# Tanh to SBUF buffers of its own in a fused attention and gated convolution kernel, with a mask on TensorE, three weight loads, halved V shifts and a new order

## The chip, the cores and the metric

The kernel runs on one core of a Trainium2 chip. The metric is device time in microseconds (us). Runs of one kernel differ (those of the kernel before lay between 226.52 and 231.59 us), so each version was run several times beside the kernel before, on the same chip. A run counts as slow if it is over 1.5% above the fastest of the same kernel. "Granted clock" is the share of full speed that TensorE's clock was given.

In the profile PE is TensorE's matmuls, PEld its weight loads, DVE is VectorE, ACT is ScalarE, POOL is GpSimd and SP is SyncE, which issues the DMAs.

## The reference

Eight batches, eight heads, 576 positions, head size 64: attention in a window of 32 to each side, then a feed-forward layer with a depthwise convolution of three taps along the sequence and a gate.

```python
scores = scale * q @ k.T                  # kept where abs(i - j) <= 32
x = (softmax(scores) @ v)                 # heads side by side: 8 x 576 x 512
h = np.maximum(x @ w_in, 0.0)             # 8 x 576 x 1024
conv_out = sum(conv_w[k] * hp[:, k:k + S, :] for k in range(3))
gate = 1.0 / (1.0 + np.exp(-conv_out))
out = h * gate @ w_out
```

Since 1/(1+exp(-x)) = (1 + tanh(x/2))/2, the kernel keeps hT = h/2 in bf16, convolves that, and forms (tanh + 1) * hT.

## The kernel before: the parts that matter

The sequence is cut into twelve chunks of 384 positions, each in eight tiles of 128 features. One chunk is cut into halves of 192, so there are 88 long units and 16 short ones, 104 in all. A unit goes: projection on TensorE into PSUM, relu into SBUF (hT), three taps shared out among TensorE, VectorE and GpSimd with the sum in a PSUM bank (pc, shown as pf in the profile), tanh on ScalarE, gate on VectorE into gT, output projection on TensorE.

```python
def emit_tanh(e_):                        # PSUM -> the same PSUM bank
    scalar.activation(pc.ap[:, 0:nc_], pc.ap[:, 0:nc_], AF.Tanh, bias=0.0, scale=1.0)

def emit_gate(e_):                        # (tanh + 1) * hT: one input in PSUM, one in SBUF
    vector.scalar_tensor_tensor(
        out=gT.ap[...], in0=in3(pc.ap), scalar=1.0, in1=taps(1), op0=ALU.add, op1=ALU.mult)
```

Two more kinds of VectorE instruction matter for the comparison, both with two inputs in SBUF: a tap that starts from a GpSimd product, and the mask of the attention.

```python
def emit_times(e_, cp, kk):               # GpSimd: cp = tap weight * hT, SBUF -> SBUF
    gpsimd.tensor_scalar(out=in3(cp.ap), in0=taps(kk), scalar1=w_tap(kk), ...)

def emit_tap(e_, kk, from_):              # VectorE: from_ is pc (PSUM) or cp (SBUF)
    vector.scalar_tensor_tensor(out=in3(pc.ap), in0=taps(kk), scalar=w_tap(kk), in1=in3(from_.ap), ...)

def emit_mask(e_, x=x):                   # VectorE or GpSimd: attn = attn * mask
    (vector if e_ == "V" else gpsimd).tensor_tensor(out=at_.ap[...], in0=at_.ap[...], in1=mask, op=ALU.mult)
```

All instructions are emitted in the order of one table, which names the engine and the buffer of each; filler matmuls on a tile of zeros are set into it at the start. The kernel uses eight PSUM banks, in turns. `cp` is GpSimd's tap buffer, `vo` is V shifted by 64 positions, `ve` V as loaded and cast, `qkb` the cast q and k, `xn` the normalised attention output.

The softmax here doesn't subtract the row's maximum and nothing guards it: scores larger than these inputs give would overflow.

## Time and profile before

| | before |
|---|---|
| time, median of 3 runs | 228.67 us (227.7 to 229.04) |
| span of the profiled run | 225.6 us |
| VectorE busy, GpSimd busy | 197.3 us, 137.7 us |
| the 104 gates | 52.1 us of VectorE |

```profile
PEld L232 <- DVE gT L232: 0.9, 2, 0.5
```

### The profile page before, as it was taken

Reading aid. Unit: us, or ns where it says so; the run is one execution under the profiler, and the core shown is the slowest. Engines: PE = TensorE matmul, PEld = TensorE weight load, DVE = VectorE, ACT = ScalarE, POOL = GpSimd, SP = SyncE. Lnnn points to the kernel's source line nnn. Section 1 sums busy time; section 2 is a strip of 40 time slices with the busy share of each in tenths; the row PEclk is TensorE's granted clock in tenths of the full one; section 3 lists DMA queues with packets and bytes.
Section 4 is the critical chain, followed back from the end, with each engine's and each line's share of the span. In section 5 each row is a group of like instructions: output and inputs, shape, how many; then the busy total and the mean of one; then the engine's idle time right before and its main releaser. Section 6 shows DMA issues by size and latency. Waiting matters only on the chain.

```text
span 225.6 us, 7189 instructions
## 1 busy us (share of the span) xinstructions
PE 211.5 (94%) x2720; PEld 122.9 (54%) x2720; DVE 197.3 (87%) x467; ACT 187.5 (83%) x474; POOL 137.7 (61%) x203
## 2 busy tenths in 40 slices
PE   7698899989989999989999998999999999999993
PEld 5366567658555655545555454545655565455541
DVE  6279869899999979797999788989999999899990
ACT  2689899998989889879889989689989999777642
POOL 5978654654376937695368736756386735566640
PEclk9889999999999999999999999999999999999999
DMA  6999999999989999999997989994535212501224
GB/s 201 331 285 358 355 266 281 321 308 253 290 170 324 317 175 287 236 306 224 288 347 129 202 278 358 182 231 147 144 36 118 99 46 49 175 1 49 93 101 178
DMA packets 66391, 48.16 MB, mean 214 GB/s; under 512 B 50781, under 2 KB 50805, under 8 KB 66357
## 3 DMA queue, kind: packets, MB, share of 16 engines
q1 hardware_dynamic: 64992, 46.32, 78.6%
q10 hardware_dynamic: 1364, 1.39, 2.9%
q8 instruction: 21, 0.34, 0.8%
q14 instruction: 14, 0.11, 0.2%
HBM read 32.52 MB, written 9.44 MB: 186 GB/s over the span
## 4 chain that ended last, share of the span: by engine, by line
PE 41%; DVE 18%; ACT 17%; DMA 13%; issue 5%; SPq 3%; POOL 2%; DVEq 0%; ACTq 0%; POOLq 0%
PE pf L232 41%; DMA st<-in_k_dram 7%; ACT attn L232 6%; DVE pf L232 5%; DVE gT L232 4%; SPq L232 3%; DMA out_dram<-y 3%; ACT xn L232 3%; DVE qkT L232 2%; ACT pf L232 2%; DMA vo<-ve 2%; DVE attn L232 2%; DVE xn L232 2%; ACT qkb L232 2%; ACT y L232 1%
## 5 line engine op out<-in xcount | busy, mean ns | idle before, releaser
L232 PE MATMUL pf<-xT,w_in_sb 128*128 128x385 bf16 (+2 forms) x416 | 73.4, 315 | 3.6 <-ACT hT L232 0.9
L232 PE MATMUL pf<-w_out_sb,gT 128*128 128x512 bf16 x288 | 72.2, 380 | 0.0
L232 POOL TENSOR_SCALAR cp<-hT,conv_w_sb 128x384 f32<-128x384 bf16 (+1 forms) x63 | 38.9, 622 | 46.1 <-ACT hT L232 20.2
L232 ACT ACTIVATE pf<-pf 128x384 f32<-128x384 f32 (+1 forms) x104 | 48.2, 477 | 13.1 <-DVE pf L232 11.1
L232 DVE SCALAR_TENSOR_TENSOR gT<-pf,hT 128x384 bf16<-128x384 f32 (+1 forms) x104 | 52.1, 517 | 5.5 <-ACT pf L232 5.1
L232 PEld LDWEIGHTS <-w_in_sb 128*128 128x128 bf16 x416 | 38.6, 98 | 27.8 <-issue 4.5
L232 ACT ACTIVATE attn<-pf 128x512 bf16<-128x512 f32 (+1 forms) x96 | 41.4, 522 | 1.8 <-PE pf L232 1.8
L232 ACT ACTIVATE hT<-pf 128x385 bf16<-128x385 f32 (+2 forms) x76 | 35.4, 487 | 6.0 <-PE pf L232 5.6
L232 PEld LDWEIGHTS <-gT 128*128 128x128 bf16 x288 | 26.0, 98 | 25.7 <-DVE gT L232 0.5
L232 DVE SCALAR_TENSOR_TENSOR pf<-hT,conv_w_sb,pf 128x384 f32<-128x384 bf16 (+1 forms) x61 | 34.7, 586 | 1.2 <-PE pf L232 1.1
L232 PE MATMUL pf<-hT,diag_w 128*128 128x384 bf16 (+1 forms) x153 | 30.9, 309 | 0.9 <-DVE xn L232 0.6
L232 POOL TENSOR_SCALAR qkb<-st 128x1152 bf16<-128x1152 f32 (+1 forms) x23 | 25.7, 1122 | 7.6 <-DMA st<-in_k_dram 3.2
L232 DVE COPY qkT<-pf 128x576 bf16<-128x576 bf16 x35 | 25.6, 750 | 4.9 <-PE pf L232 4.9
L232 POOL TENSOR_TENSOR cp<-cp,cp 128x384 f32<-128x384 f32 (+1 forms) x24 | 24.4, 1016 | 1.6
L232 DVE TENSOR_TENSOR attn<-attn,mask 128x1152 bf16<-128x1152 bf16 x26 | 23.0, 886 | 2.4 <-ACT attn L232 2.3
L232 ACT ACTIVATE xn<-pf,rec 128x64 bf16<-128x64 f32 x96 | 22.0, 360 | 1.5 <-DVE rec L232 1.5
L232 ACT COPY y<-pf 128x512 f32<-128x512 f32 x30 | 18.1, 605 | 3.9 <-PE pf L232 3.7
L232 DVE SCALAR_TENSOR_TENSOR pf<-hT,conv_w_sb,cp 128x384 f32<-128x384 bf16 (+1 forms) x35 | 21.2, 618 | 0.0
L232 POOL TENSOR_TENSOR attn<-attn,mask 128x1152 bf16<-128x1152 bf16 x6 | 14.2, 2371 | 8.4 <-ACT attn L232 8.4
L232 DVE TENSOR_TENSOR xn<-pf,rec 128x256 bf16<-128x256 f32 x48 | 18.9, 410 | 0.0
L232 ACT COPY qkT<-pf 128x576 bf16<-128x576 bf16 x29 | 18.6, 664 | 0.4 <-PE pf L232 0.2
L232 PEld LDWEIGHTS <-diag_w 128*128 128x128 bf16 x153 | 13.3, 97 | 9.8 <-issue 1.3
(49 smaller groups left out, 235.2 us busy)
## 6 DMA issues: line engine op xcount, KB each, us to landing
st<-in_q_dram SPq DMA_DIRECT2D x16, 576.0 KB, 6.8
out_dram<-y SPq DMA_DIRECT2D x36, 256.0 KB, 3.8
st<-in_k_dram SPq DMA_DIRECT2D x14, 576.0 KB, 8.2
vst<-in_v_dram SPq DMA_DIRECT2D x24, 256.0 KB, 7.0
vst<-in_v_dram SPq DMA_DIRECT2D x15, 192.0 KB, 5.7
vo<-ve SPq DMA_DIRECT2D x11, 260.0 KB, 5.6
st<-in_moe_w_in_dram SPq DMA_DIRECT2D x2, 1024.0 KB, 9.3
st<-in_moe_w_out_dram SPq DMA_DIRECT2D x2, 1024.0 KB, 9.4
```

Source lines behind the costliest of these rows:

```text
L232: return lambda *args, **kwargs: fixed(do(*args, **kwargs))
```

## The change

The intent is to free a PSUM bank at the tanh's end instead of at the gate's end, to take work off VectorE and GpSimd, and to shorten the start. The core of the diff:

```diff
-BUFS = {'st': 3, ..., 'rec': 4, 'xn': 3, 'hT0': 8, 'hT1': 6, 'hT2': 6, 'cp': 2, 'gT': 4, 'y': 7}
+BUFS = {'st': 4, ..., 'rec': 8, 'xn': 2, 'hT0': 7, 'hT1': 7, 'hT2': 7, 'cp': 2, 'gT': 3, 'y': 5, 'tn': 3}
+MASKS = ('aa', 'mm', 'mm', 'mm', 'mm', 'mm', 'mm', 'mm')
 (CONV, who computes which tap, TURNS and ORDER: new tables)
+    tn_p = pool("tn", [128, CH], FP32)
...
-            scalar.activation(pc.ap[:, 0:nc_], pc.ap[:, 0:nc_], AF.Tanh, bias=0.0, scale=1.0)
+            scalar.activation(tn.ap[:, 0:nc_], pc.ap[:, 0:nc_], AF.Tanh, bias=0.0, scale=1.0)
...
-                ..., in0=in3(pc.ap), scalar=1.0,
+                ..., in0=in3(tn.ap), scalar=1.0,
                 in1=taps(1), op0=ALU.add, op1=ALU.mult,
...
+                if added:                 # first batch: the mask is added to the scores on TensorE
+                    for n, e, width in ((2, x, 2), (0, 0, 8), (1, 1, 8)):
+                        tensor.matmul(ps[n].ap[...], outside[rows, :], ident[...], start=True, stop=False)
...
+    W_PARTS = {"in": ((0, 2), (2, 4), (4, MB)), "out": ((0, MB // 2), (MB // 2, MB))}
...
-        for c in range(NBLK - 1) if b < 2 else (0,):
-            shift_v(b, c, c + 1 if b < 2 else NBLK - 1)
+        for c in range(0, NBLK - 1, 1 if b < 2 else 2):
+            shift_v(b, c, c + (1 if b < 2 else 2))
```

## The prediction

What the prediction calls the lock is its assumption that a VectorE instruction with two SBUF inputs and a GpSimd instruction hold each other up. Of the trace of before it had the mask, which has two SBUF inputs: the ten masks that started with a GpSimd instruction running for 0.1 us or more took 1104 ns, the other 16 took 750. The gates, with one input in PSUM and one in SBUF, took 548 ns beside a GpSimd instruction (79 of the long ones) and 550 without (9). The rows by form bear on whether an SBUF source is quicker than PSUM, and the "starts 216 ns apart" are those of matmuls. On the blur that it mentions: of the 64-row matmuls of 64 columns, 498 of 1098 starts came under 5 ns after the one before.

> **What bounds the kernel now.** I read the page's busy shares first, then the windows by stage, the chain of waits, the groups by form, and last the order of time around single instructions. The busy shares:
>
> ```profile
> PE 211.5 (94%) x2720; PEld 122.9 (54%) x2720; DVE 197.3 (87%) x467; ACT 187.5 (83%) x474; POOL 137.7 (61%) x203
> ...
> DMA  6999999999989999999997989994535212501224
> ```
>
> No engine is idle on average, so the shares alone decide nothing; the stages do. The windows (length, then busy time of PE, PEld, DVE, ACT, POOL, then granted clock, DMA share and GB/s):
>
> ```profile
> 10.00:20.00 10.00, 9.68 (x177) 6.78 (x174) 7.37 (x12) 9.32 (x22) 8.07 (x18) 0.84 1.06 303
> 20.00:30.00 10.00, 8.89 (x124) 5.74 (x122) 8.27 (x27) 8.83 (x28) 7.41 (x9) 1.00 1.08 368
> ...
> 60.00:100.00 40.00, 37.80 (x575) 21.23 (x575) 37.00 (x88) 34.69 (x84) 29.79 (x29) 1.00 1.04 254
> 100.00:140.00 40.00, 38.12 (x536) 21.36 (x537) 35.01 (x83) 36.55 (x97) 24.21 (x29) 1.00 1.07 262
> 140.00:190.00 50.00, 50.00 (x634) 27.49 (x633) 48.84 (x110) 43.85 (x116) 30.66 (x38) 1.00 0.54 120
> 190.00:220.00 30.00, 29.50 (x155) 14.91 (x154) 28.52 (x56) 20.19 (x46) 16.94 (x24) 1.00 0.26 86
> ```
>
> Until about 26 us PE looks busy but mostly runs the 75 filler matmuls; ScalarE works through the first exponentials. From 30 to 140 us PE, VectorE, ScalarE and the DMA engines are all near full. From 140 us on PE and VectorE are full and the DMA is not. The chain of waits (start, length, what) says the same:
>
> ```profile
> 16.40 2.95 ACT attn L232 x7
> 19.38 0.76 DVE attn L232
> ...
> 20.89 0.67 DVE attn L232
> 21.61 0.33 PE pf L232 x6
> ...
> 83.06 4.46 DMA vo<-ve
> ...
> 136.25 48.21 PE pf L232 x603
> ...
> 194.01 27.28 PE pf L232 x142
> ```
>
> A first stage ends in the exponentials and two masks on VectorE; a middle changes hands often, once through a DMA that shifts V; the last 85 us are PE alone but for a short stretch at 185 to 194.
>
> How much of PE can be won? I measured the spacing of matmul starts. Taking each kind's quick quarter as its pace and counting what lies over 60 ns beyond it, PE stands for 17.6 us between 30 and 140 us, and for only 4.4 us after 140. Pairs of 64-row matmuls blur this by some us. So the gain must come from the first 140 us.
>
> [...] The gate reads one tensor of PSUM now[...]; after the change it reads tn and hT, both in SBUF. [...]
>
> ```profile
> 85.31 1.03 DVE L232 TENSOR_TENSOR attn<-attn,mask 128x1152 bf16<-128x1152 bf16 x1
> ...
> 85.12 0.62 POOL L232 TENSOR_SCALAR ve<-vst 128x512 bf16<-128x512 f32 x1
> ```
>
> GpSimd ends at 85.74 and the mask 0.60 us later; undisturbed masks took 0.75 us. [...]
>
> ```profile
> L232 DVE SCALAR_TENSOR_TENSOR gT<-pf,hT 128x384 bf16<-128x384 f32 x88 | 46.8, 548 | 5.4 <-ACT pf L232 5.1
> L232 ACT ACTIVATE pf<-pf 128x384 f32<-128x384 f32 x88 | 42.8, 498 | 12.7 <-DVE pf L232 10.9 <-DVE rec L232 1.1 <-PE pf L232 0.2
> L232 ACT ACTIVATE hT<-pf 128x385 bf16<-128x385 f32 x47 | 23.3, 510 | 4.6 <-PE pf L232 4.2
> L232 DVE TENSOR_TENSOR attn<-attn,mask 128x1152 bf16<-128x1152 bf16 x26 | 23.0, 886 | 2.4 <-ACT attn L232 2.3
> L232 DVE SCALAR_TENSOR_TENSOR pf<-hT,conv_w_sb,cp 128x384 f32<-128x384 bf16 x33 | 20.4, 630 | 0.0
> ```
>
> Tanh into PSUM and relu of nearly the same size into SBUF differ by 12 ns; a tap with both inputs in SBUF (630) isn't quicker than one that reads PSUM (613). So I give the gate no saving. [...] starts 216 ns apart at 512 columns, 163 at 384, 56 at 128 (medians).
>
> **The change part by part.** The order of both programs gives the counts; durations are means of the table by form.
>
> PE: 21 more tap matmuls of 384 columns and 3 of 192: 21 x 163 + 3 x 83 = +3.7 us. Ten fewer transposes of 128 columns: -0.6. The first batch's mask becomes 8 matmuls of 512 and 4 of 128 columns added into the scores: 8 x 216 + 4 x 56 = +2.0 us, where PE has only fillers to run, so hidden. Fillers fall from 75 to 39, which frees idle time only. On the path: +3.1 us, about half of it (10 of the taps, 1.6 us) in the chunks of the full second half.
>
> VectorE: taps -7.4 us (4 x 613, 4 x 630, 6 short ones), 13 fewer qkT copies at 750 = -9.8, masks -1.8, V casts -2.2, relus and xT copies -2.6; more y copies +2.7, xn +1.2, early casts and diagonals about +4.9, cp sums +0.7. Sum -14 us. ScalarE: 13 qkT copies at 664 = +8.6, 12 fewer xn at 360 = -4.3, 4 fewer y = -2.4, the rest about -2, tanh 104 x 12 ns = +1.2: near +1. GpSimd: 13 fewer cp at 622, 9 fewer cp sums at 1034, 2 fewer masks at 2371, against 10 half shifts at about 1.05 us (from 0.64 us for 520 and 1.92 for 2080 elements) and small ones: about -9.
>
> The lock: 26 masks took 886 on average against 750 undisturbed, +136 each. The 33 long taps with two SBUF inputs took only 15 more than undisturbed ones. For 104 gates that is 1.6 to 14 us of VectorE; I take 8. VectorE then keeps 6 us of its relief.
>
> PSUM: by pairing each tanh with its gate, a bank stays held 1.10 us on average from the tanh's end to the gate's end: 104 x 1.10 = 114 us of 8 x 225.6 = 1805 bank-us, 6%. That is freed.
>
> First stage: the last exponential ends at 19.35 and the values' matmuls go on at 21.61, behind two masks, a V cast and reciprocals. Without the masks I take 2.0 of these 2.3 us. The smaller first w_in load helps only if the first projection, at 25.8 us, then waits for it; the casts from 18.5 us on say it barely does.
>
> V's shift: in batches 2 to 7 each side went in one copy, 11 by DMA and 1 by GpSimd; now each goes in two halves, 10 by GpSimd, 4 by VectorE and 10 by DMA. The hole at 83 to 88 us (about 1.2 us of PE standing), where the chain waits for such a DMA, may close. The load ring grows from 3 to 4 buffers, but xn, gT and y shrink (3 to 2, 4 to 3, 7 to 5), which could make new waits; the page of before shows none on them, so I count neither.
>
> Sum: -2.0 (start) + 3.1 (PE) - 5 (standing PE won back from the 17.6 us, by freed banks, the lighter VectorE, a fourth load buffer and the shift) = -3.9 us, to 228.7 - 3.9 = 224.8 us. The 5 is my judgement, a little over a quarter of what stands; nothing in the trace gives it.
>
> **The rivals.** First, the lock takes the relief back: every gate blocked as the masks are, 14 us, and GpSimd's own reads blocked by gates. For it: 79 of the 88 long gates overlap a GpSimd instruction in the trace. Against: the taps with two SBUF inputs mostly fall into gaps of GpSimd, and GpSimd gets lighter. It would give 228 to 232. Second, PE is the bound and nothing else matters: it pays the added 3.1 us, less the start: about 229. For it: the 48 and 27 us of PE in the chain. Against: 17.6 us of standing before 140. Third, the new order closes most of the holes, winning 10 us of them: about 220. For it: every resource but ScalarE is relieved and a whole table was made anew. Against: ScalarE, at 8.7 of 10 us and more from 30 to 140, is not relieved.
>
> **Range and chances.** The second rival and a mild lock bound it above, the third below: 219.5 to 230 holds it 8 times in 10. Two per cent faster is 224.1, just under my figure, so faster by over 2% has 0.42, within 2% 0.52, slower 0.06.
>
> **What would show it.** The first projection matmul starts about 2 us earlier; tap matmuls read 24 more; PE's standing between 30 and 140 us falls to some 12 us. Gates in SBUF keep a shortest duration near 520 ns with a mean near 600 or 650; a mean of 700 is the first rival. VectorE's busy time stays near 190 us. I am wrong if the start isn't earlier, if VectorE rises over 200 us, or if PE's holes stay as they are (then same) or nearly vanish (then clearly faster).

## More of the kernel before

The chain that ended last, by engine, in the kernel before:

```profile
PE 41%; DVE 18%; ACT 17%; DMA 13%; issue 5%; SPq 3%; POOL 2%; DVEq 0%; ACTq 0%; POOLq 0%
```

Two wide windows of it (length, then busy time and count of PE, PEld, DVE, ACT, POOL, then granted clock, DMA share, GB/s), and how long TensorE's weight loads waited for a gate (us in total, times, longest):

```profile
30.00:140.00 110.00, 104.95 (x1574) 63.03 (x1574) 99.92 (x242) 100.02 (x260) 67.39 (x76) 1.00 1.08 266
140.00:220.00 80.00, 79.50 (x787) 42.40 (x786) 77.36 (x165) 64.04 (x160) 47.60 (x61) 1.00 0.44 107
```

## The result, and the profile after

| | before | after |
|---|---|---|
| time, median of 4 runs each | 228.77 us (227.7 to 229.04) | 242.31 us (242.01 to 243.71) |
| span of the profiled run | 225.6 us | 240.3 us |
| VectorE busy, GpSimd busy | 197.3, 137.7 us | 209.0, 143.0 us |
| the 104 gates | 52.1 us | 70.8 us |

The changed kernel is slower: ratio 1.0613, with a 95% interval of 1.0559 to 1.0667. A ratio here is the mean time of one kernel's fast runs over that of the other's of the same rounds, so it is not quite the ratio of the medians. All four runs of the changed kernel, the profiled one included, were fast, and from 30 us on the granted clock is 1.00 in both profiles. The prediction, 224.8 us in a range of 219.5 to 230, missed in size and in direction; it had given "slower" a chance of 0.06.

The busy shares and the chain by engine of the kernel after:

```profile
PE 216.5 (90%) x2710; PEld 124.2 (52%) x2710; DVE 209.0 (87%) x448; ACT 187.9 (78%) x470; POOL 143.0 (60%) x198
...
DVE 39%; PE 27%; DMA 12%; ACT 9%; POOL 5%; issue 5%; SPq 1%; POOLq 0%; DVEq 0%; ACTq 0%
```

VectorE runs 19 instructions fewer than before (448 against 467) and is busy 11.7 us longer. It has taken the chain over from TensorE. The same two wide windows after the change:

```profile
30.00:140.00 110.00, 101.02 (x1474) 60.23 (x1473) 101.00 (x205) 95.26 (x248) 74.10 (x79) 1.00 1.00 242
140.00:220.00 80.00, 77.44 (x846) 42.57 (x844) 76.58 (x160) 65.94 (x169) 45.65 (x49) 1.00 0.49 122
```

Between 30 and 140 us VectorE is as busy as before, but gets through 205 instructions where it got through 242, and TensorE through 100 matmuls fewer. The table of groups says which instructions grew (line, engine, operation, tiles, shapes and count, then busy us and mean ns of one, then idle before and its releaser). Before:

```profile
L232 POOL TENSOR_SCALAR cp<-hT,conv_w_sb 128x384 f32<-128x384 bf16 (+1 forms) x63 | 38.9, 622 | 46.1 <-ACT hT L232 20.2
```

After:

```profile
L233 DVE SCALAR_TENSOR_TENSOR gT<-tn,hT 128x384 bf16<-128x384 f32 (+1 forms) x104 | 70.8, 699 | 2.1 <-ACT tn L233 1.5
L233 POOL TENSOR_SCALAR cp<-hT,conv_w_sb 128x384 f32<-128x384 bf16 (+1 forms) x53 | 41.3, 783 | 47.4 <-ACT hT L233 21.2
```

The gates took 18.7 us more. GpSimd's taps grew too, from 622 to 783 ns each, so ten fewer of them still take 2.4 us more. One gate and the GpSimd instructions around it, in order of time (start, length), VectorE first:

```profile
102.18 1.32 DVE L233 SCALAR_TENSOR_TENSOR gT<-tn,hT 128x384 bf16<-128x384 f32 x1
103.43 0.61 DVE L233 SCALAR_TENSOR_TENSOR pf<-hT,conv_w_sb,pf 128x384 f32<-128x384 bf16 x1
```

```profile
102.09 1.00 POOL L233 TENSOR_TENSOR cp<-cp,cp 128x384 f32<-128x384 f32 x1
103.06 1.45 POOL L233 TENSOR_SCALAR qkb<-st 128x1152 bf16<-128x1152 f32 x1
```

The gate starts 0.09 us after a GpSimd sum, which ends at 103.09. The gate ends 0.41 us after that, at 103.50: about three quarters of its usual 0.55 us came once GpSimd had finished. The tap after it reads PSUM, and takes its usual 0.61 us beside the next GpSimd instruction.

I paired every gate of 384 columns with the GpSimd instruction running at its start. Of 88 gates, 38 ended 0.40 to 0.42 us after that GpSimd instruction; they took 940 ns on average. The other 50 took 546 ns. Eighteen of these 50 also started with a GpSimd instruction marked as running; in seven cases it had at most 0.05 us left, and in eleven it was that instruction which ended late, 0.37 to 0.92 us after the gate. So whichever of the two came second waited for the other to end.

Part of what VectorE lost can be seen at TensorE as waits of weight loads for a gate, 0.9 us before and now:

```profile
PEld L233 <- DVE gT L233: 7.8, 13, 1.5
```

By the spacing of matmul starts, as the prediction measured it, TensorE stands 23.0 us between 30 and 140 us (17.6 before) and 9.3 us after 140 (4.4 before). That accounts for the span: +10.3 us of standing, +0.7 of a later first projection (26.54 against 25.80 us) and the +3.1 of added matmuls make 14.1 of the 14.7 us. It is an account of one profile of each kernel, and the 3.1 is the prediction's estimate.

The start, in a window and in the chain of waits:

```profile
10.00:20.00 10.00, 7.70 (x142) 5.11 (x134) 4.76 (x13) 6.34 (x15) 7.39 (x15) 0.58 0.99 250
```

```profile
11.72 5.11 DMA vo<-ve
```

The chain no longer passes through the masks, but through the first half shift of V, which now goes by DMA. The granted clock fell to 0.58 there (0.84 before) in this run. One profile of a start says little: experiments 2, 5 and 10 keep the order of the changed kernel, and their first projections start at 24.88, 25.38 and 25.12 us (clock 0.83, 1.00 and 0.83 in that window). Experiments 1 and 6 have the start of the kernel before, and theirs come at 26.53 and 26.83 us, in profiles of runs that counted as slow. So the 0.7 us can't be put down to the change.

### The profile page after: what moved, and what is told of

It is laid out like the page before. It is cut to its first block, busy times and chain, and to the rows that moved or that the text cites. A ratio compares the mean times of both kernels' runs of the same rounds, so it can differ in the third digit from the quotient of the medians.

```text
span 240.3 us, 7118 instructions
## 1 busy us (share of the span) xinstructions
PE 216.5 (90%) x2710; PEld 124.2 (52%) x2710; DVE 209.0 (87%) x448; ACT 187.9 (78%) x470; POOL 143.0 (60%) x198
## 4 chain that ended last, share of the span: by engine, by line
DVE 39%; PE 27%; DMA 12%; ACT 9%; POOL 5%; issue 5%; SPq 1%; POOLq 0%; DVEq 0%; ACTq 0%
PE pf L233 27%; DVE gT L233 13%; DVE pf L233 12%; DMA st<-in_q_dram 6%; DVE xn L233 3%; ACT tn L233 3%; POOL cp L233 3%; DMA st<-in_k_dram 2%; DVE qkT L233 2%; POOL qkb L233 2%; DMA vo<-ve 2%; DVE attn L233 2%; ACT xn L233 2%; DMA vst<-in_v_dram 2%; DVE hT L233 2%
## 5 line engine op out<-in xcount | busy, mean ns | idle before, releaser
L233 DVE SCALAR_TENSOR_TENSOR gT<-tn,hT 128x384 bf16<-128x384 f32 (+1 forms) x104 | 70.8, 699 | 2.1 <-ACT tn L233 1.5
L233 ACT ACTIVATE tn<-pf 128x384 f32<-128x384 f32 (+1 forms) x104 | 49.2, 491 | 24.2 <-DVE pf L233 18.2
L233 PE MATMUL pf<-hT,diag_w 128*128 128x384 bf16 (+1 forms) x177 | 36.0, 310 | 0.9 <-DVE hT L233 0.3
L233 DVE SCALAR_TENSOR_TENSOR pf<-hT,conv_w_sb,pf 128x384 f32<-128x384 bf16 (+1 forms) x52 | 30.5, 600 | 1.5 <-PE pf L233 1.3
L233 POOL TENSOR_SCALAR qkb<-st 128x1152 bf16<-128x1152 f32 (+2 forms) x22 | 26.7, 1219 | 6.6 <-PE pf L233 4.3
L233 ACT COPY qkT<-pf 128x576 bf16<-128x576 bf16 x42 | 26.4, 665 | 1.6 <-PE pf L233 1.5
L233 POOL TENSOR_SCALAR vo<-ve 64x1040 bf16<-64x1040 bf16 (+1 forms) x18 | 17.9, 994 | 12.4 <-ACT ve L233 6.9
L233 POOL TENSOR_SCALAR ve<-vst 128x512 bf16<-128x512 f32 x22 | 16.9, 776 | 5.6 <-DMA vst<-in_v_dram 5.4
L233 PEld LDWEIGHTS <-qkT 64*128 64x128 bf16 x576 | 13.3, 98 | 12.7 <-issue 11.1
L233 PE MATMUL pf<-ident,qkb 64*128 64x64 bf16 x576 | 15.2, 192 | 5.0 <-DVE y L233 1.4
```

What stands on the lines that cost most here:

```text
L233: return lambda *args, **kwargs: fixed(do(*args, **kwargs))
```

## The experiments

Ten kernels ran. The theory was the waiting that the pairing above shows: the gate now has two inputs in SBUF and waits for GpSimd, or makes it wait. The rivals were the new order, the start, the shift of V by GpSimd, and the mere writing and reading of fp32 in SBUF.

### 1. Only the tanh moved, in the order of before

```diff
-            scalar.activation(pc.ap[:, 0:nc_], pc.ap[:, 0:nc_], AF.Tanh, bias=0.0, scale=1.0)
+            tn_of[u] = tn_free.pop(0)
+            scalar.activation(tn_b[tn_of[u]][:, 0:nc_], pc.ap[:, 0:nc_], AF.Tanh, bias=0.0, scale=1.0)
...
-                ..., in0=in3(pc.ap), scalar=1.0,
+                ..., in0=in3(tn_b[tn_of[u]]), scalar=1.0,
```

There are four tanh buffers, and two xn buffers instead of three so that they fit. Nothing else differs from the kernel before; four entries of the order table name another xn buffer.

> The kernel before with its own order; only the tanh goes to SBUF (four fp32 buffers, xn reduced from 3 to 2 buffers to make room). Lock theory: gates that overlap a GpSimd instruction rise from 548 to some 750 ns, VectorE's busy time rises by 10 to 20 us, and the program takes 233 to 242 us against 228.7. Order theory (the new order and the added PE work are to blame): within 1% of the kernel before, 227 to 231 us.

Measured: 249.41 us (246.27 to 252.03), ratio 1.0849 (1.0757 to 1.0941). That is slower than the 233 to 242 us I expected: the part alone costs more than the whole change. Two of the four runs counted as slow. The profiled run counted as slow (250.68 us), so its spans aren't compared; its rows show where the time lies:

```profile
L230 DVE SCALAR_TENSOR_TENSOR gT<-tn,hT 128x384 bf16<-128x384 f32 (+1 forms) x104 | 74.5, 733 | 2.4 <-ACT tn L230 2.2
L230 POOL TENSOR_SCALAR cp<-hT,conv_w_sb 128x384 f32<-128x384 bf16 (+1 forms) x63 | 51.8, 826 | 50.2 <-DVE pf L230 18.1
...
DVE 55%; PE 14%; ACT 10%; issue 9%; POOL 7%; DMA 3%; ACTq 0%; SPq 0%; DVEq 0%; POOLq 0%
```

In the same order as before, 104 gates took 22.4 us more and the GpSimd taps 12.9 us more. The new order, the loads and the start are not needed for the loss. In the new order the loss is smaller: there 49 of the 88 long gates start while a GpSimd instruction has 0.1 us or more to run, here 57. Whether that is why isn't shown; without the second input the rest of the change wins nothing (experiments 5 and 9).

### 2. Half of the tanhs back into PSUM, in the order of after

```diff
-        tn = Slot(tn_p)
+        tn = pc if at in BACK else Slot(tn_p)      # BACK: 51 units
```

BACK holds the 51 units whose PSUM bank isn't taken again before their gate, so that the order need not move. In the other 53 it is taken before the gate.

> The changed kernel with the same order; the 51 of 104 tanh results whose PSUM bank isn't taken by anything else before the gate go back into that bank. Lock theory: those 51 gates fall back to 548 ns, VectorE's busy time falls by 7 to 12 us, and the program takes 233 to 238 us against 242.3. Order theory: within 1% of the changed kernel, 240 to 244 us.

Measured: 240.55 us (238.94 to 242.83), ratio 1.0534 (1.0462 to 1.0605): less won than I expected.

```profile
L284 DVE SCALAR_TENSOR_TENSOR gT<-tn,hT 128x384 bf16<-128x384 f32 (+1 forms) x53 | 36.2, 693 | 0.6 <-ACT tn L284 0.5
L284 DVE SCALAR_TENSOR_TENSOR gT<-pf,hT 128x384 bf16<-128x384 f32 (+1 forms) x51 | 24.8, 500 | 4.7 <-ACT pf L284 4.3
```

Within one kernel, gates that read PSUM are short and gates that read SBUF are long (547 against 686 ns at 384 columns); VectorE fell to 201.6 us and GpSimd to 134.0. But the time fell by only 0.8 points, and the two intervals overlap. These 51 units hold their banks to the gate's end again, which may give back what VectorE won; I didn't separate the two, and it stays open.

### 3. The first half shift of V by VectorE instead of a DMA

```diff
-33D
+33V        # one entry of the order table
```

> The changed kernel, but the first 64-row shift of V of the first batch is a VectorE copy, as in the kernel before, and not a DMA. If the start is held by that DMA (5.1 us in the chain, with PE standing 1.1 us behind it and a granted clock of 0.58 from 10 to 20 us), the first projection starts 1 to 2 us earlier and the program takes 239 to 241.5 us. If the start is hidden by what comes later: within 0.5 us of 242.3.

Measured: 243.39 us (242.05 to 244.94), ratio 1.0684 (1.0615 to 1.0753). The first projection starts at 24.59 us instead of 26.54, but with the DMA left in it started at 24.88 to 25.38 us in experiments 2, 5 and 10, so most of the 2 us isn't shown to come from the edit. The time isn't shorter, and VectorE leads the chain here too (46% of it, TensorE 23%).

### 4. The ten GpSimd half shifts of V by DMA

```diff
-(ten entries "vo hi" / "vo lo" of batches 2 to 7 on G)
+(the same entries on D)
```

> The changed kernel, but the ten half shifts of V by GpSimd in batches 2 to 7 go by DMA. GpSimd loses 11.8 us of busy time that reads SBUF. Lock theory: gates overlap GpSimd less, VectorE's busy time falls by 2 to 5 us, and the program gains 1 to 4 us (238 to 241). Rival: the DMA's landing time of 4 us and more makes the values wait, and it is as slow or slower (242 to 246).

Measured: 254.43 us (252.73 to 257.17), ratio 1.1141 (1.1064 to 1.1219): 12 us worse, a miss. GpSimd got lighter (130.5 us), and still the kernel lost: in this order a shift by DMA can land late (the twenty half shifts of 130 KB took 4.4 us from issue to landing, the median). One of them alone held TensorE for 8.2 us (wait, us in total, times, longest; below it the row of the gates). The gates are as long as in the changed kernel (699 ns there), and VectorE fell by 1.3 us only, to 207.7:

```profile
PE pf L232 <- DMA vo<-ve: 8.2, 1, 8.2
...
L232 DVE SCALAR_TENSOR_TENSOR gT<-tn,hT 128x384 bf16<-128x384 f32 (+1 forms) x104 | 70.4, 696 | 2.4 <-ACT tn L232 1.8
```

So the long gates don't come from the shifts by GpSimd. What those shifts cost in time this kernel can't tell, as the DMAs brought a wait of their own.

### 5. The order of after, with a gate that reads the tanh alone

```diff
-            vector.scalar_tensor_tensor(
-                out=gT..., in0=in3(tn.ap), scalar=1.0, in1=taps(1), op0=ALU.add, op1=ALU.mult,
+            vector.tensor_scalar(
+                out=gT..., in0=tn..., scalar1=1.0, scalar2=0.25, op0=ALU.add, op1=ALU.mult,
```

The result is wrong (hT is left out). The tanh is still written to SBUF as fp32 and read from there; a small gap every 128 columns was put in, meant to keep the instruction at its usual pace. Its 543 ns at 384 columns are near the 548 of before; what it takes without the gap wasn't measured.

> The changed kernel with the same order and the same tanh to SBUF; only the gate reads one SBUF tensor in place of two (tn plus one, times a constant[...]; the result is wrong on purpose). Lock theory: every gate takes about 550 ns, GpSimd's taps fall from 783 to some 640 ns, and the program takes 226 to 233 us. If tanh in SBUF or the longer order is to blame by itself: 239 to 243 us.

Measured: 231.58 us (231.13 to 235.08), ratio 1.0154 (1.0088 to 1.022).

```profile
L233 DVE TENSOR_SCALAR gT<-tn 128x384 bf16<-128x384 f32 (+1 forms) x104 | 51.5, 512 | 4.9 <-ACT tn L233 4.3
L233 POOL TENSOR_SCALAR cp<-hT,conv_w_sb 128x384 f32<-128x384 bf16 (+1 forms) x53 | 33.2, 631 | 48.5 <-ACT hT L233 29.2
...
PE 67%; DMA 9%; DVE 7%; ACT 6%; issue 4%; POOL 4%; SPq 1%; DVEq 0%; ACTq 0%; POOLq 0%
```

With one SBUF input the gate of 384 columns takes 543 ns on average: 542 where a GpSimd instruction overlaps it, 544 where none does. VectorE falls from 209.0 to 188.2 us and GpSimd from 143.0 to 129.3, and TensorE leads the chain again. The second SBUF input of the gate accounts for 4.6 of the 6.1 points (1.0613 less 1.0154, each against before in its own batch). In this batch, that of experiments 5 to 7, four of the seven runs of the kernel before counted as slow (230.62 to 231.59 us), and the record calls its verdicts unclear. The ratios rest on the other three, 226.91 to 228.55 us; against all seven, experiment 5 would come out closer to before still.

### 6. The order of before, with the same one-input gate

The diff is that of experiment 1 with the gate of experiment 5. Its output is wrong, which doesn't matter for the time.

> The kernel before with its own order and the tanh in SBUF as in the first experiment (249 us), but the gate reads one SBUF tensor (result wrong on purpose). Lock theory: 225 to 230 us, the kernel before within 1%. If writing tanh to SBUF or reading it from there costs by itself: 235 us or more.

Measured: 228.36 us (227.21 to 231.34), ratio 0.9989 (0.9913 to 1.0064). The profiled run counted as slow (231.34 us), the other four were fast.

```profile
L230 DVE TENSOR_SCALAR gT<-tn 128x384 bf16<-128x384 f32 (+1 forms) x104 | 51.8, 513 | 8.0 <-ACT tn L230 7.4
```

Experiment 1 and this one differ in the gate's second input, and in what comes with leaving it out (another VectorE instruction, the gap in the tanh's buffer): 8.5% slower against no difference that shows. Writing the tanh to SBUF, reading it there and the smaller xn pool cost nothing that shows, and freeing the PSUM banks earlier won nothing that shows in that order.

### 7. The order of after, with all tanhs back in PSUM

```diff
-        tn = Slot(tn_p)
+        tn = pc
```

Since 53 banks are taken again before their gate, the order had to be sorted anew: 125 of 452 entries of TensorE, 46 of VectorE's and 45 of ScalarE's are in another place.

> The changed kernel with all 104 tanh results back in their PSUM banks; where an instruction of the old order took such a bank before its gate, it is moved behind the gate (some 125 of 452 TensorE steps shift). Lock theory: all gates at 548 ns, 230 to 238 us, some of the gain given back because banks are held longer. Order theory: 240 us or more.

Measured: 269.72 us (267.51 to 270.29), ratio 1.1816 (1.1716 to 1.1916): a clear miss.

```profile
PE pf L231 <- DVE gT L231: 16.3, 25, 1.8
```

VectorE is busy only 191.1 us here, but matmuls wait for gates to free their banks. That suggests that the new order leans on early freed banks. This kernel isn't a clean undoing, since the order moved too, so nothing more is read from it.

### 8. The kernel before, with the first batch's masks added on TensorE

```diff
+                added = b == 0
+                if added:
+                    (three matmuls of `outside` by `ident` into the scores' banks, as in the change)
...
             def emit_mask(e_, x=x):
+                if b == 0:
+                    return
```

> The kernel before with one part of the change alone: the four masks of the first batch are added on TensorE ahead of the scores, and VectorE's four multiplications of that batch are gone; order, buffers and everything else are as before. If the masks of the first batch are on the path that sets the start, as the prediction had it (2.0 us), the first projection starts up to 2 us before 25.8 us and the time is 226 to 228. Rival: TensorE's fillers and the loads set the start, the first projection stays within 0.5 us and the time within 0.5% of before (228 to 229.5). I lean to the rival, because the changed kernel, which has this part too, began its first projection later and not earlier.

Measured: 227.45 us (226.29 to 228.94, 6 runs) against 228.44 (226.52 to 230.8, 11 runs), ratio 0.9981 (0.9933 to 1.0029). The first projection starts at 26.70 us, not earlier than 25.80; by the spread of starts told above the difference isn't one. The chain of this kernel in the start:

```profile
9.24 5.52 PE pf L232 x87
...
17.45 3.12 ACT attn L232 x8
20.56 1.00 ACT w_in_sb L232 x2
21.57 1.66 ACT xn L232 x8
```

The exponentials of that stage that began at 16.40 us before begin at 17.45 now, though the granted clock was 1.00 in that window (0.84 before). They stand behind 5.5 us of TensorE, with six of the mask matmuls among its 87, and after them ScalarE's weight cast and normalisation set the pace. The mask matmuls stand on the chain here, not beside it, and another wait took the masks' place.

### 9. Experiments 5 and 3 together

The diff is both of theirs. Its output is wrong, which doesn't matter for the time.

> The changed kernel with the gate that reads the tanh alone (a wrong result on purpose, as before) and the first shift of V by VectorE instead of a DMA. The gate alone left it 1.5% over before (231.6). If the late start is what is left of the loss, this gives 229 to 230.5; if the rest is in TensorE's added work and in the new order, it stays at 231 to 232.5. I expect the second with 60%.

Measured: 229.97 us (227.84 to 233.78, 6 runs), ratio 1.004 (0.9974 to 1.0107). I had leaned to 231 to 232.5. That may suggest that the start holds the rest of the loss, but the first projection begins at 25.38 us both here and in experiment 5, and the intervals of the two ratios touch. The chain of the start shows another limit by now:

```profile
12.83 7.72 DMA st<-in_moe_w_in_dram
```

So without the second SBUF input the changed kernel comes to between the same time and 2% more than before; how that rest divides among order, added matmuls and start stays open.

### 10. The tanh as bf16, in the order of after

```diff
-    tn_p = pool("tn", [128, CH], FP32)
+    tn_p = pool("tn", [128, CH], BF16)
```

> The changed kernel with the tanh as bf16 instead of fp32 in its own SBUF buffers; the gate still reads two operands of SBUF. If what costs is the reading of two SBUF operands beside GpSimd, whatever their type, gates of 384 columns that meet GpSimd stay near 780 ns and the time at 239 to 243. If it is the fp32 traffic, the gates alone come under 500 ns and the time falls to 232 to 237. I expect the first with 75%.

Measured: 243.59 us (240.76 to 245.0), ratio 1.0601 (1.0517 to 1.0684).

```profile
L233 DVE SCALAR_TENSOR_TENSOR gT<-tn,hT 128x384 bf16<-128x384 bf16 (+1 forms) x104 | 71.0, 701 | 2.1 <-ACT tn L233 1.5
```

Half the tanh's bytes, the same loss: 37 gates waited for GpSimd and took 953 ns, the other 51 took 547. Two of the four runs counted as slow; the fast ones took 240.76 and 242.64 us, within the 239 to 243 I expected. It is the number of SBUF inputs that counts here, not the size of the tanh.

No version ran that beats the kernel before; the nearest, experiment 8, can't be told from it.

## Why the prediction was wrong, point by point

**The step that failed** is "The lock: ... For 104 gates that is 1.6 to 14 us of VectorE; I take 8. VectorE then keeps 6 us of its relief." The wait was named; its size was wrong. Measured between the changed kernel and experiment 5, the second input costs VectorE 20.8 us (209.0 less 188.2), of which the gates are 19.3 (70.8 less 51.5), above the upper end of the bracket. And the sum left a term out: "GpSimd's own reads blocked by gates" stands in the first rival without a figure. It measured 13.7 us of GpSimd (143.0 less 129.3).

**Why the size was wrong.** The bracket averaged two kinds of instruction by their means. A mean hides how often the case arises. The masks' +136 is the mean of ten that waited (1104 ns) and 16 that didn't (750). In the trace of before, only 5 of the 33 long taps with two SBUF inputs start while a GpSimd instruction has 0.1 us or more to run; those 5 took 710 ns on average, the other 28 about 616. Of the long gates, 57 of 88 start in that case. The taps' +15 ns came from an order in which they rarely meet GpSimd.

**It could have been had blind.** The ten masks that started under a running GpSimd instruction before ended 0.60 to 0.62 us after it, 0.145 us less than an undisturbed mask takes (0.75). So the loss of one is what GpSimd still has to run, less about 0.145 us. Summed over the 104 gates of before, by where each starts, that is 28.5 us; an estimate of mine made afterwards from that trace, and an upper one, since an order that stretches moves the meetings. Experiment 1 measured 22.4 us (in a profile of a run that counted as slow by its time, with a clock of 0.969).

**The relief of 14 us on VectorE** was too large: without the second input VectorE has 188.2 us, 9.1 under before. The relief of 9 us on GpSimd was near: 8.4. With the true loss VectorE ends 11.7 us above where it started, and it was at 37 of 40 us in the window from 60 to 100 already. So there was little room to absorb it.

**"-2.0 (start)"** didn't show. The first projection came 0.7 us later in the profiled pair; over all profiles named above it came at 24.88 to 26.54 us with the new order and at 25.80 to 26.83 with the start of before, so a gain of a part of the 2 us may hide in that spread. Experiment 8 shows no earlier start from the masks alone: the mask matmuls, which the prediction took as hidden behind fillers, stood on the chain there. And the earliest start, 24.59 us in experiment 3, came with no shorter time.

**"-5 (standing PE won back)"** never came: TensorE's standing rose by 10.3 us. Experiment 6 shows that earlier freed banks in the order of before win nothing visible, so the 6% of bank time that was freed had no one waiting for it there.

**"+3.1 (PE)"** is consistent with the span's account, but no run isolates it.

**The rivals.** The first had the right cause and too small a result: "228 to 232" against 242.3. It took 14 us as the most that VectorE could lose and didn't add what GpSimd loses, nor that VectorE would become the chain. The second, TensorE alone with "about 229", is near what experiments 5 and 9 measure (231.6 and 230.0) once the gate's second input is gone. The third, "about 220", came in no run.

**Its own tests** were good: "a mean of 700 is the first rival" was met with 699, and "if VectorE rises over 200 us" with 209.0.

## What to carry to other kernels

Before an operand moves from PSUM to SBUF, count the SBUF inputs of the VectorE instruction that reads it. With a second one, it and GpSimd's instructions took turns here: 38 of 88 long gates ended 0.40 to 0.42 us after a GpSimd instruction and took 940 ns, against 546 for the others. With one SBUF input the gate took 542 ns beside GpSimd and 544 without (experiment 5).

Size that from the trace of the kernel at hand, by where each such instruction would start and what GpSimd then still has to run (less about 0.14 us here, for gates as for masks), and not from the mean of other instructions in luckier places. And charge it to both engines: here the gates lost 19.3 us and GpSimd 13.7, and relief elsewhere covered neither.

In the profile the wait stood inside the duration of the instruction that waited, on both engines: gates of 940 ns, and GpSimd taps of 783 ns on average instead of 622, the longest 1.74 us. So VectorE's busy time rose from 197.3 to 209.0 us with 19 instructions fewer.

Nor did the move itself pay here: gates that ran beside no GpSimd instruction took 547 ns with the tanh in SBUF, those of the kernel before 548 with it in PSUM. A PSUM bank is held 1.10 us on average from the tanh's end to its gate's end in the kernel before; freeing it earlier won nothing that shows (ratio 0.9989 in experiment 6), and moving the tanh cost 8.5% where the gate got a second SBUF input by it (experiment 1).
